# Sliding-window decode attention with a gated MLP: a quarter of the last Wo head group loaded in nine partial-row transfers, and the copy of x loaded on SyncE's queue

## The chip, the cores and the metric

The kernel runs on one core of one Trainium2 chip. The metric is device time in microseconds (us) of one launch. The kernel before was timed in three runs: 198.23, 198.25 and 198.52 us, median 198.25. The profile that is read below comes from one further execution, which took 198.21 us.

## The reference

One decode step for a batch of 8 rows of width 512. The input is normalised, goes through attention over the last 2048 positions of a key/value cache (32 query heads, 8 key/value heads of width 128) and, beside it, through a gated MLP of inner width 1792. The output is x + s * silu(b).

```python
xn = _layernorm(x, axis=-1)
# attention: W = min(4096, max(256, Sk // 4)) = 2048 of Sk = 8192
q = (xn @ wq).reshape(B, Sq, Hq, Dh)                 # 8 x 512 @ 512 x 4096
k, v = the last W positions of k_cache, v_cache, each head used by 4 query heads
p = softmax(q . k * Dh ** -0.5);  o = p . v
s = o.reshape(B, Sq, Hq * Dh) @ wo                   # 8 x 4096 @ 4096 x 512
# MLP
h = sigmoid(xn @ w_gate) * (xn @ w_up)
b = h @ w_down
out = x + s * silu(b)
```

Everything is bf16 in memory. Keys and values of the window are 32 MB each, the weights wq and wo 4 MB each, the MLP's three weights 1.75 MB each: about 81 MB are read for 8 KB of output.

## The kernel before, in words

**Loads.** All large loads go through `load` (line 88), which issues a DMA on SyncE's queue (`nc.sync`, SP in the profile). Keys and values come in tiles of 2 MB (`load_kv`, line 110), 16 of each; the query weights in two tiles; the MLP's in three. All of them live in a ring of nine buffers (`ring`, `RING = 9`). The list `loads` (lines 138 to 146) fixes their order: keys in the order of use, each value tile a lag behind its keys, the MLP's gate and up weights ahead of the last two tiles, and at the end the down weight and the two halves of Wo, `(2, 2), (3, 0), (3, 1)`. `issue_loads` (line 164) walks this list and stops where the buffer of nine places earlier is not in `released` yet. It is called after each step of the main loop, so a transfer is issued on the chip when the work on the buffer's former contents has ended.

**Marks of the transfers.** The framework gives each DMA that SyncE or ScalarE issues one of eight semaphores (marks) in turn: the first is `x_bf` on ScalarE's queue, then the loads on SyncE's, at the end the two stores of the output, one on each queue. A transfer that takes a mark waits, on the queue that issues it, until the transfer that had the mark before has landed. So each transfer waits for the one eight places earlier. DMAs of GpSimd's queue have marks of their own.

**Wo.** `wo_view` (line 149) has eight head groups (`hg`), 128 rows (`p`) and four quarters (`j`) of 512 columns: one row of one quarter is 1 KB, one quarter of a head group 128 KB. `load_wo` (line 152) loads the first half as two pieces of two head groups (1 MB each) and the second as head groups 4, 5 and 6 (512 KB each), quarters 0 and 1 of head group 7 (256 KB), quarter 2 (128 KB) and quarter 3 (128 KB), in this order.

**The copy of x.** `x2_sb` (line 181) is a 64 x 256 tile in the layout of the last sum: GpSimd clears it and then issues two DMAs of 8 rows by 512 B on its own queue (line 184), near the kernel's start.

**The end.** The main loop (line 610) interleaves the scores, softmax and value products of the 16 tiles. After it come the last sums of heads, `o_rows(1)`, the MLP's output product (`unit_out`, line 338) and the product with Wo (line 658 on): `order` runs through the head groups and their quarters, for each two matmuls (one for each half of the columns) accumulate into `a_ps`. VectorE then multiplies with the gate (`prod`, line 673) and adds `x2_sb` (`y_bf`, line 675), and two DMAs store the output (line 677). At the very end SyncE waits for all marks one after the other and a barrier follows (line 706 in the profile, the end of the context).

Of the kernel before, what the change touches and what calls it, by code (L numbers as in the profile page):

```python
# [10 lines left out]
def kernel(  # L11
# [13 lines left out]
    nc = tc.nc  # L25
    P = 128
    B, _, D = A_x.shape
# [9 lines left out]
    HG = Hq // 4  # L37
# [24 lines left out]
    NCOL = 2  # L62
    DC = D // NCOL

    bf16 = mybir.dt.bfloat16
# [8 lines left out]
    work = ctx.enter_context(tc.tile_pool(name="work", bufs=1))  # L74
# [13 lines left out]
    def load(dst, src, q=None):  # L88
        if q is None:
            q = nc.sync  # L90
        q.dma_start(out=dst, in_=src)

    def ring_tile(shape, name):
        return ring.tile(shape, bf16, name=name, tag="ring", align_bytes=ALIGN)

    x_bf = work.tile([B, D], bf16, name="x_bf")
    nc.scalar.dma_start(out=x_bf[:], in_=A_x.flatten_outer_dims())

# [3 lines left out]
    for kh in range(2):  # L102
        t = ring_tile([P, KH, Hq * Dh], f"wq_sb{kh}")
# [45 lines left out]
    wo_view = A_wo.rearrange("(hg p j) n -> p hg j n", p=P, j=4)  # L149
    wo_parts = {}  # L150

    def load_wo(half):
        t = ring_tile([P, HG // 2, 4, D], f"wo_sb{half}")
        for h0, h1, j0, j1 in (
            ((0, 2, 0, 4), (2, 4, 0, 4)),
            ((4, 5, 0, 4), (5, 6, 0, 4), (6, 7, 0, 4), (7, 8, 0, 2), (7, 8, 2, 3), (7, 8, 3, 4)),
        )[half]:
            o = half * (HG // 2)
            load(t[:, h0 - o : h1 - o, j0:j1, :], wo_view[:, h0:h1, j0:j1, :])
            for hg in range(h0, h1):  # L160
                for j in range(j0, j1):
                    wo_parts[hg, j] = t[:, hg - o, j, :]

    def issue_loads():
        while loads_done[0] < len(loads):
            n = loads_done[0]
            if n >= RING and loads[n - RING] not in released:
                break
            kind, i = loads[n]
            if kind == 0:  # L170
                k_tiles[i] = load_kv(A_k_cache, i, "k_sb")
            elif kind == 1:
                v_tiles[i] = load_kv(A_v_cache, i, "v_sb")
            elif kind == 2:
                load_mlp(i)
            else:
                load_wo(i)
            loads_done[0] += 1

    issue_loads()  # L180
    x2_sb = work.tile([NCOL * 32, DC], bf16, name="x2_sb")
    nc.gpsimd.memset(x2_sb[:], 0.0)
    for j in range(NCOL):
        nc.gpsimd.dma_start(
            out=x2_sb[32 * j : 32 * j + B, :],
            in_=A_x.flatten_outer_dims()[:, DC * j : DC * (j + 1)],
        )

    ident = consts.tile([P, P], bf16, name="ident")
    make_identity(nc, ident[:])  # L190
# [18 lines left out]
        out=rstd[:], in_=mv[:, 1:2], func=AF.Sqrt, bias=eps_t[:], scale=1.0  # L209
# [4 lines left out]
        out=xn_bf[:],  # L214
# [7 lines left out]
    for kt in range(KT):  # L222
        nc.tensor.transpose(
            out=xnT_ps[:, kt, :], in_=xn_bf[:B, kt::KT], identity=ident[:B, :B]
# [8 lines left out]
    for off in range(-rep * (NQ - 1), rep * NQ, rep):  # L233
        nc.gpsimd.affine_select(
            out=SumM[:],
            in_=SumM[:],
# [9 lines left out]
        out=SumM_blk,  # L246
        in_=SumM_blk,
# [7 lines left out]
        out=SumM_blk,  # L255
        in_=SumM_blk,
# [11 lines left out]
        out=Jneg[:],  # L268
        in_=ident[:].rearrange("p (a j r) -> p j a r", j=NQ, r=rep),
# [4 lines left out]
        out=Jneg[:], in0=Jneg[:], scalar1=-scale, scalar2=None, op0=ALU.mult  # L274
# [4 lines left out]
        out=Hm[:],  # L279
        in_=ident[:].rearrange("p (a gl) -> p gl a", gl=GL),  # L280
# [5 lines left out]
    for w in (32, 64):  # L286
        Sel[w] = consts.tile([P, w], f32, name=f"Sel{w}")
        nc.vector.tensor_reduce(
            out=Sel[w][:],
            in_=ident[:].rearrange("p (a m) -> p m a", m=w),  # L290
# [7 lines left out]
    for Q in range(NQ):  # L298
        nc.vector.tensor_copy(
            out=spread[:, :, Q, 32 * Q : 32 * (Q + 1)].rearrange(  # L300
                "m c (k g) -> m c g k", g=GL
            ),
            in_=ident[:].rearrange("m (g c k) -> m c g k", c=C4, k=KQ),
# [353 lines left out]

    a_ps = psum.tile([NCOL * 32, DC], f32, name="a_ps", tag="wide")
    order = [(hg, j) for hg in range(HG) for j in range(4)]
    for n, (hg, j) in enumerate(order):  # L660
        for c in range(NCOL):
            nc.tensor.matmul(  # L662
                a_ps[32 * c : 32 * (c + 1), :],
                lhsT=o2_sb[:, hg, j, :],
                rhs=wo_parts[hg, j][:, DC * c : DC * (c + 1)],
                start=(n == 0),
                stop=(n == len(order) - 1),
                tile_position=(0, 32 * c),
                skip_group_check=True,
            )  # L670
# [5 lines left out]
    for c in range(NCOL):  # L676
        queues[c].dma_start(
            out=out.flatten_outer_dims()[:, DC * c : DC * (c + 1)],
            in_=y_bf[32 * c : 32 * c + B, :],
# [31 lines left out]
```

## Time and profile before

| what | us |
|---|---|
| median of three runs | 198.25 |
| the profiled execution | 198.21 |
| its span, first to last instruction | 196.5 |
| the rest, outside the span | 1.7 |
| busy: TensorE matmuls | 138.2 |
| busy: VectorE | 117.0 |
| busy: ScalarE | 32.6 |
| busy: GpSimd | 9.3 |
| DMA from 13 to 155 us: share of the 16 engines, rate | 1.01, 430 GB/s |
| DMA from 183 to 193 us | 0.91, 363 GB/s |

A busy time is the sum over an engine's own work; the DMA share is the mean over the core's 16 DMA engines, and a share of 1 over a stretch says that none of them stood idle in it. The chain is the path of releases followed back from the last instruction. Issuing a DMA takes time on the queue of the engine that issues it (SPq for SyncE's), which is not counted as busy. Beside the views, the trace holds a record of each DMA packet (its start, duration and size) and the moment of each increment of a transfer's mark: a transfer over 128 rows increments its mark 16 times, once for each of the 16 engines, and has landed with the last.

### The profile page before, as it was taken

Reading aid. Unit: us, or ns where it says so; the run is one execution under the profiler, and the core shown is the slowest. Engines: PE = TensorE matmul, PEld = TensorE weight load, DVE = VectorE, ACT = ScalarE, POOL = GpSimd, SP = SyncE. Lnnn points to the kernel's source line nnn. Section 1 sums busy time; section 2 is a strip of 40 time slices with the busy share of each in tenths; the row PEclk is TensorE's granted clock in tenths of the full one; section 3 lists DMA queues with packets and bytes.
Section 4 is the critical chain, followed back from the end, with each engine's and each line's share of the span. In section 5 each row is a group of like instructions: output and inputs, shape, how many; then the busy total and the mean of one; then the engine's idle time right before and its main releaser. Section 6 shows DMA issues by size and latency. Waiting matters only on the chain.

```text
span 196.5 us, 2699 instructions
## 1 busy us (share of the span) xinstructions
PE 138.2 (70%) x1112; PEld 57.6 (29%) x1112; DVE 117.0 (60%) x200; ACT 32.6 (17%) x68; POOL 9.3 (5%) x21
## 2 busy tenths in 40 slices
PE   0340078669998987899789278946794779674783
PEld 0110011032324222423333044404240424443661
DVE  3818999746686828664777277837773750361101
ACT  3008540410121102101210021002100210340000
POOL 8820000000000000000000000000000000000000
PEclk9999999955999997879999957996888587996579
DMA  6999999999999999999999999999999999999991
GB/s 215 429 427 427 430 434 429 440 434 427 434 427 434 427 427 427 430 434 430 430 434 434 424 427 440 430 425 427 430 434 430 427 431 434 423 424 420 411 391 41
DMA packets 6860, 81.19 MB, mean 413 GB/s; under 512 B 792, under 2 KB 1088, under 8 KB 2112
## 3 DMA queue, kind: packets, MB, share of 16 engines
q1 hardware_dynamic: 6752, 81.01, 97.1%
q8 instruction: 8, 0.13, 0.2%
q10 hardware_dynamic: 32, 0.01, 0.1%
q14 instruction: 4, 0.03, 0.0%
q0 software_dynamic: 64, 0.01, 0.0%
HBM read 81.02 MB, written 0.01 MB: 412 GB/s over the span
## 4 chain that ended last, share of the span: by engine, by line
DMA 72%; DVE 17%; PE 8%; ACT 1%; issue 1%; SPq 0%; DVEq 0%; ACTq 0%
DMA k_sb<-in_A_k_cache_dram 47%; DMA wd_sb<-in_B_w_down_dram 14%; DVE k_sb L422 11%; DMA wq_sb<-in_A_wq_dram 6%; DMA wo_sb<-in_A_wo_dram 5%; PE pT_ps L486 3%; PE s_ps L435 3%; DVE qz_sb L395 2%; PE acc_ps L549 1%; DVE mx L447 1%; DVE qT_sb L386 1%; DVE pt_bf L475 1%; ACT L461 1%; PE q_ps L367 1%; PE mb_ps L456 0%
## 5 line engine op out<-in xcount | busy, mean ns | idle before, releaser
L422 DVE STREAM_TRANSPOSE k_sb<-k_sb 128x1024 f32<-128x1024 f32 x64 | 75.9, 1219 | 16.6 <-DMA k_sb<-in_A_k_cache_dram 16.5
L435 PE MATMUL s_ps<-k_sb,qz_sb 128*32 128x512 bf16 x256 | 68.7, 1065 | 16.4 <-DVE k_sb L422 11.6
L549 PE MATMUL acc_ps<-v_sb,pT_sb 128*32 128x256 bf16 (+1 forms) x416 | 35.3, 345 | 3.9 <-DMA v_sb<-in_A_v_cache_dram 2.6
L549 PEld LDWEIGHTS <-pT_sb 128*32 128x32 bf16 (+1 forms) x416 | 12.5, 109 | 33.2 <-issue 27.0
L506 DVE TENSOR_SCALAR pT_sb<-pc_bf,Hm 128x512 bf16<-128x512 bf16 x32 | 9.1, 349 | 18.3 <-ACT pc_bf L495 18.3
L435 PEld LDWEIGHTS <-qz_sb 128*32 128x32 bf16 x256 | 8.3, 100 | 34.0 <-issue 26.1
L560 ACT COPY acc_sb<-acc_ps 128x256 f32<-128x256 f32 (+1 forms) x16 | 7.2, 453 | 63.2 <-PE acc_ps L549 63.2
L486 PE MATMUL pT_ps<-pt_bf,spread 128*128 128x128 bf16 x128 | 12.5, 272 | 6.3 <-DVE pt_bf L475 6.3
L570 PEld LDWEIGHTS oT_ps<-Sel,acc_sb 128*128 128x128 f32 x88 | 11.8, 202 | 14.3 <-ACT acc_sb L560 8.5
L570 PE MATMUL oT_ps<-Sel,acc_sb 128*128 128x16 f32 x88 | 13.4, 276 | 1.1 <-ACT acc_sb L560 1.1
L486 PEld LDWEIGHTS <-spread 128*128 128x128 bf16 x128 | 10.8, 123 | 10.8 <-DVE pt_bf L475 10.8
L456 PE MATMUL mb_ps<-mj,SumM 128*128 128x4 f32 x16 | 3.5, 286 | 14.3 <-DVE mj L449 14.3
L461 ACT ACTIVATE p_bf<-s_ps,nm 128x512 bf16<-128x512 f32 x8 | 5.5, 687 | 46.5 <-DVE nm L458 46.5
L577 DVE TENSOR_TENSOR oT_sb<-oT_ps,rden 128x16 bf16<-128x16 f32 x16 | 2.6, 160 | 11.7 <-PE oT_ps L570 11.7
L456 PEld LDWEIGHTS mb_ps<-mj,SumM 128*128 128x128 f32 x16 | 2.8, 218 | 22.5 <-DVE mj L449 20.6
L397 ACT COPY qz_sb<-qT_sb 32x128 bf16<-32x128 bf16 x20 | 8.3, 413 | 3.0 <-DVE qT_sb L386 2.7
L530 DVE RECIPROCAL rden<-den_ps 128x32 f32<-128x32 f32 x8 | 2.8, 351 | 7.3 <-PE den_ps L528 7.3
L495 ACT CAST pc_bf<-pT_ps 128x512 bf16<-128x512 f32 x8 | 4.7, 587 | 13.1 <-PE pT_ps L486 13.1
L367 PE MATMUL q_ps<-wq_sb,xnT_sb 128*32 128x512 bf16 x32 | 3.8, 625 | 4.0 <-DMA wq_sb<-in_A_wq_dram 4.0
L475 DVE STREAM_TRANSPOSE pt_bf<-p_bf 128x512 bf16<-128x512 bf16 x8 | 5.4, 679 | 1.9 <-ACT p_bf L461 1.9
L662 PE MATMUL a_ps<-wo_sb,o_sb 128*32 128x256 bf16 x64 | 5.5, 315 | 1.0 <-DMA wo_sb<-in_A_wo_dram 0.9
L447 DVE TENSOR_REDUCE mx<-s_ps 128x1 f32<-128x512 f32 x8 | 5.3, 657 | 0.0
(61 smaller groups left out, 61.9 us busy)
## 6 DMA issues: line engine op xcount, KB each, us to landing
k_sb<-in_A_k_cache_dram SPq DMA_DIRECT2D x16, 2048.0 KB, 31.8
v_sb<-in_A_v_cache_dram SPq DMA_DIRECT2D x16, 2048.0 KB, 29.5
wq_sb<-in_A_wq_dram SPq DMA_DIRECT2D x2, 2048.0 KB, 9.7
wo_sb<-in_A_wo_dram SPq DMA_DIRECT2D x2, 1024.0 KB
wg_sb<-in_B_w_gate_dram SPq DMA_DIRECT2D x1, 1792.0 KB, 29.3
wu_sb<-in_B_w_up_dram SPq DMA_DIRECT2D x1, 1792.0 KB, 30.1
wd_sb<-in_B_w_down_dram SPq DMA_DIRECT2D x1, 1792.0 KB, 27.6
wo_sb<-in_A_wo_dram SPq DMA_DIRECT2D x3, 512.0 KB, 23.5
```

The costliest lines, as they stand in the source:

```text
L397: nc.scalar.copy(out=out, in_=in_)
L422: nc.vector.transpose(out=kw, in_=kw)
L435: nc.tensor.matmul(s_tiles[b][32 * gl : 32 * (gl + 1), :], lhsT=qz_sb[:, b, GL * gg + gl, j, :], rhs=kT[:, :, a, :, gl, e], start=(gg == 0 ...
L447: nc.vector.reduce_max(out=mx[:], in_=s_tiles[b][:], axis=AX.X)
L456: nc.tensor.matmul(mb_ps[:], lhsT=SumM[:], rhs=mj[:], start=True, stop=True)
L461: nc.scalar.activation(out=p_bf[:], in_=s_tiles.pop(b)[:], func=AF.Exp, bias=nm[:], scale=scale, accum_out=den128[:],)
L475: nc.vector.transpose(out=pt_bf[:].rearrange("p c g q r -> p (c g q r)"), in_=p_bf[:])
L486: nc.tensor.matmul(pT_ps[:, :, c4, :], lhsT=spread[:, c4, Q, :], rhs=pt[:, :, Q, :], start=(Q == 0), stop=(Q == NQ - 1), skip_group_check= ...
L506: nc.vector.tensor_scalar(out=pT_tiles[b][:, :, gl, :], in0=pc, scalar1=Hm[:, gl : gl + 1], scalar2=None, op0=ALU.mult,)
L549: nc.tensor.matmul(acc_tiles[i][w * c : w * (c + 1), :], lhsT=pT[:, 32 * y : 32 * y + w], rhs=v_tiles[i][:, ch : ch + n_ch, :].rearrange(" ...
L560: nc.scalar.copy(out=acc_sb[:], in_=acc_tiles.pop(i)[:])
L570: nc.tensor.matmul(oT_ps[:], lhsT=acc_sb[:, Dh * c : Dh * (c + 1)], rhs=sel[:, c // 2, c % 2], start=(c == 0), stop=(c == n_ch - 1),)
```

## The change

Quarter 2 of head group 7 (128 rows of 1 KB) is no longer one transfer after head group 7's first half. It is cut into nine transfers of 64, 14, 12, 10, 8, 8, 6, 4 and 2 rows. Three of them follow head group 4, three head group 5 and three head group 6. Quarters 0 and 1 and then quarter 3 of head group 7 are the last two pieces. The product with Wo takes head group 7's quarters in the order 2, 0, 1, 3. The two DMAs of `x2_sb` move from GpSimd's queue at the start to SyncE's queue, between the two pieces of Wo's first half; GpSimd still clears the tile, now as its first work.

```diff
+    x2_sb = work.tile([NCOL * 32, DC], bf16, name="x2_sb")
+    nc.gpsimd.memset(x2_sb[:], 0.0)
     x_bf = work.tile([B, D], bf16, name="x_bf")
...
+    def load_x2():
+        for j in range(NCOL):
+            load(
+                x2_sb[32 * j : 32 * j + B, :],
+                A_x.flatten_outer_dims()[:, DC * j : DC * (j + 1)],
+            )
+
+    PARTS = (64, 14, 12, 10, 8, 8, 6, 4, 2)
+
     def load_wo(half):
         t = ring_tile([P, HG // 2, 4, D], f"wo_sb{half}")
-        for h0, h1, j0, j1 in (
-            ((0, 2, 0, 4), (2, 4, 0, 4)),
-            ((4, 5, 0, 4), (5, 6, 0, 4), (6, 7, 0, 4), (7, 8, 0, 2), (7, 8, 2, 3), (7, 8, 3, 4)),
-        )[half]:
-            o = half * (HG // 2)
-            load(t[:, h0 - o : h1 - o, j0:j1, :], wo_view[:, h0:h1, j0:j1, :])
-            for hg in range(h0, h1):
-                for j in range(j0, j1):
-                    wo_parts[hg, j] = t[:, hg - o, j, :]
+        h_lo = half * (HG // 2)
+
+        def piece(h0, h1, j0, j1, r0=0, r1=P):
+            load(
+                t[r0:r1, h0 - h_lo : h1 - h_lo, j0:j1, :],
+                wo_view[r0:r1, h0:h1, j0:j1, :],
+            )
+
+        if half == 0:
+            piece(0, 2, 0, 4)
+            load_x2()
+            piece(2, 4, 0, 4)
+        else:
+            r0 = 0
+            for n, rows in enumerate(PARTS):
+                if n % 3 == 0:
+                    h = h_lo + n // 3
+                    piece(h, h + 1, 0, 4)
+                piece(HG - 1, HG, 2, 3, r0, r0 + rows)
+                r0 += rows
+            assert r0 == P
+            piece(HG - 1, HG, 0, 2)
+            piece(HG - 1, HG, 3, 4)
+        for h in range(h_lo, h_lo + HG // 2):
+            for j in range(4):
+                wo_parts[h, j] = t[:, h - h_lo, j, :]
...
-    x2_sb = work.tile([NCOL * 32, DC], bf16, name="x2_sb")
-    nc.gpsimd.memset(x2_sb[:], 0.0)
-    for j in range(NCOL):
-        nc.gpsimd.dma_start(
-            out=x2_sb[32 * j : 32 * j + B, :],
-            in_=A_x.flatten_outer_dims()[:, DC * j : DC * (j + 1)],
-        )
...
     order = [(hg, j) for hg in range(HG) for j in range(4)]
+    order[-4:] = [(HG - 1, j) for j in (2, 0, 1, 3)]
```

## The prediction

> **What bounds the kernel now.** I read the page's rows of slices first, then the chain, then the stretches and waits of its end.
>
> The slices show DMA full from the second to the last but one:
>
> ```profile
> DMA  6999999999999999999999999999999999999991
> GB/s 215 429 427 427 430 434 429 440 434 427 434 427 434 427 427 427 430 434 430 430 434 434 424 427 440 430 425 427 430 434 430 427 431 434 423 424 420 411 391 41
> ```
>
> So the time is 81 MB at about 430 GB/s, plus what follows the last byte. The chain, from 155 us on, says which bytes count:
>
> ```profile
> 155.44 27.61 DMA wd_sb<-in_B_w_down_dram
> 183.06 9.89 DMA wo_sb<-in_A_wo_dram
> 192.95 0.04 issue
> 192.99 0.30 PE a_ps L662 x2
> 193.29 0.02 issue
> 193.32 0.42 DVE prod L673
> 193.74 0.02 issue
> 193.76 0.28 DVE y_bf L675
> ```
>
> The down weight lands at 183.05, the last quarter of Wo at 192.95; two matmuls and two VectorE operations follow, the stores are issued at 194.07, and the span ends at 196.5. Only three things can change the time: when the last piece of Wo lands, what TensorE has left then, and what follows the stores.
>
> Issues on SyncE's queue, taken from its timeline in narrow windows, show how the tail is fed:
>
> ```profile
> 165.58 0.82 SPq L91 DMA_DIRECT2D wo_sb<-in_A_wo_dram  x2
> 169.08 4.22 SPq L91 DMA_DIRECT2D wo_sb<-in_A_wo_dram  x1
> 173.93 3.39 SPq L91 DMA_DIRECT2D wo_sb<-in_A_wo_dram  x1
> 178.77 1.52 SPq L91 DMA_DIRECT2D wo_sb<-in_A_wo_dram  x1
> 183.06 0.33 SPq L91 DMA_DIRECT2D wo_sb<-in_A_wo_dram  x1
> ```
>
> The last four issues begin when the up weight, the last two value tiles and the down weight have landed (169.06, 173.92, 178.76, 183.05 by the records): each waits for the mark of the transfer eight places earlier. Here that costs nothing, since 9.9 us of data still lie ahead.
>
> Last, the 16 increments of each mark. The last quarter's come in two groups: seven engines at 191.18 to 191.64, nine at 192.54 to 192.95. The queues' rows show what makes engines late:
>
> ```profile
> q1 hardware_dynamic: 6752, 81.01, 97.1%
> q8 instruction: 8, 0.13, 0.2%
> ```
>
> Eight instruction loads of 16 KB (44, 67, 94, 111, 131, 151, 172 and 182 us) each hold one engine for 0.88 to 0.97 us and lengthen its next packet by about half a microsecond. After each, one more increment of every transfer comes about 1.4 us late. The end is set by the nine late engines.
>
> **The change part by part.** The sum starts from the profiled execution: 198.21 us, of which 196.50 span and 1.71 outside, 0.04 below the median of 198.25.
>
> *x2 off GpSimd's queue.* GpSimd loses two issues (0.65 and 0.52, 1.17 us from 1.41 us on); its setup moves up by as much. It is idle after 13 us, and the first product waits for the query weights at 13.1, so this gains nothing, and costs nothing. ScalarE's queue is not touched. The 16 packets of 512 B (27 ns each, 9 ns a completion) leave the stream at 6 us and return at 185 us: at most two rows and two completions on one engine, 0.07, out and in: 0.
>
> *x2 on SyncE's queue.* Two issues between Wo's first pieces. What waits behind them is the second piece, issued at 159.26 now. It, and the two issues, move three marks along: the second piece now waits for the gate weights (landed 164.67), head group 4 for the up weight (169.06), the next three transfers for 173.92, 178.76 and 183.05. Data issued before 155.5 lasts to 183.05, so all of this is covered. If that cover were gone, each issue would cost about 0.45.
>
> *Rows of the nine transfers.* By the packet records a 1 KB packet takes 46 ns and a completion 9. `x_bf`, 8 rows, left eight 1 KB packets and eight completions, so I take it that a transfer of fewer than 16 rows gives an engine at most one. The 64 rows give each engine four, the other eight transfers between zero and eight more, against eight now. On the engine that ends last that is -4 to +4 rows, -0.18 to +0.18, and up to eight more completions, +0.07. Nine engines of 16 are late, so a well-served one is probably among them: near the upper end, I take +0.20 between -0.18 and +0.26.
>
> The Trainium skill, page "DMA: Bandwidth & Descriptors", section on why a DMA increments its semaphore by 16, says more: from SyncE's queue a copy uses the largest number of engines up to 16 that divides its rows, always the lowest-numbered ones. By that, engines 0 and 1 get 12 rows and 14 and 15 get 4, and the sum would have +0.26 if engine 0 or 1 is late, and about -0.1 if only upper ones are. No view shows which engines are late.
>
> *Feeding the tail.* This is the part that could cost most. In places of eight, head group 5 now waits for Wo's first piece (185.44), head group 6 for head group 4, head group 7's first half for head group 5, its last quarter for the ten-row transfer. On the late engines head group 4 lands at 189.2 (189.14 now, plus x2's 0.07). SyncE then issues six in a row: head group 6, the 6, 4 and 2 rows, the first half, the last quarter. An issue of such shapes takes 0.33 to 0.43, and 0.05 lie between two, so the first half is issued four steps of 0.38 to 0.48 later, at 190.8 to 191.2. From issue to first packet an idle path took 0.79 (store, 194.07 to 194.86) to 1.04 (first weights, 0.81 to 1.85), so its data can start at 191.6 to 192.2. The late engines are free for it at about 192.0 (191.65 now is when head group 6 lands, 0.3 after its last packet; plus x2, plus up to 12 rows and nine completions less the last). Head group 6 itself, issued at 189.25, is ready at 190.3 and needed at 190.6. So the stall is 0 to 0.2; with the 0.69 of the first key issues as a step it would be 1.0. I take 0.1, near the rows of like shapes, and keep 0 to 1.0. The early engines will stand idle, which costs nothing, since they have 1.4 us to give.
>
> The same page's rules for authors say that transfers under 64 KB are mostly overhead and that two halves of the partitions should go as one transfer; its fit of 2.0 us a transfer would make nine of them about 18 us by themselves. The records here charge 9 ns a completion on an engine that has a queue, so I keep the sum above.
>
> *TensorE.* Head group 7's quarter 2 has nine transfers on six marks, so more waits stand ahead of its two matmuls: a wait instruction of TensorE took 0.05, three to five of them 0.15 to 0.25. Eight matmuls took 0.61 (at 190.45) and a pair follows a pair by 0.11. From head group 6's landing to the last one there are 1.0 to 1.3 us; 0.61, 0.25 and three pairs (0.33) make 1.2. I take +0.05, between 0 and 0.3. VectorE's wait for x2 just moves to two other marks that landed by 186.
>
> *After the stores.* The records have SyncE's seven wait instructions at the end at 194.90, 194.98, 195.05, 195.12, 195.19, 195.37 and 195.54, in the order of the marks from the second to the eighth, 0.07 apart unless one waits. The stores are the 47th and 48th transfers with such marks, so they have the seventh and eighth, landed at 195.35 and 195.53, and nothing follows but the barrier. The change adds eight pieces and two x2 transfers: the stores become 57th and 58th, with the first and second marks. If the order of waits stays, the wait of 195.53 comes first, and five more steps of 0.07 stand behind it: +0.35. If the order goes by age, 0, or -0.07 as GpSimd's two marks are gone. The order is by number as much as by age in this trace; I take +0.35 and keep -0.07.
>
> Sum: 198.21 + 0.20 + 0.10 + 0.05 + 0.35 = 198.9 us.
>
> **The rivals.**
> *Waits at the end keep the stores last* (order by age). For it: in this trace both orders agree. The sum is then 198.21 + 0.35 = 198.56, inside what a measurement can tell (0.2%, 0.4 us).
> *SyncE starves the tail.* For it: six issues in a row hang on one landing, and the first issues of this kernel took 0.63 to 0.69. Against it: rows of the same shapes took 0.33 to 0.43. Steps of 0.6 or a first packet after 1.3 us put the first half 0.4 to 1.0 late: 199.2 to 199.9.
> *The nine transfers relieve the late engines* (the other side). One mechanism: rows move from engines that an instruction load held to engines that none held. It decides if all nine late engines get at most seven rows, which spares 46 ns a row, -0.05 to -0.18, with the waits at the end unmoved and the tail fed: 198.0 to 198.2, not slower. Against it: nine late engines cannot all have fewer than eight rows unless seven take the rest, and the unevenness to be gained from is only the 0.41 within the late group. A fall of over 0.4 needs more than four rows can give.
>
> **How the numbers follow.** The forecast 0.45 (198.6 to 199.1), the tail starved 0.20 (199.2 to 199.9), the stores' waits unmoved 0.23 (198.3 to 198.6), relief 0.12 (197.8 to 198.2). Slower by over 0.2% (above 198.65) takes nearly all of the first and the second: 0.65. Within 0.2%: 0.29. Faster: half of relief's doubtful part, 0.06. The range runs from 198.1, where relief ends, to 199.7; cut off are about one in ten at each end.
>
> **What would show it.** If the steps are right, the last 16 increments of Wo come in a closer group, at 193.2 to 193.4; SyncE's issues of head group 6 and five more stand in a row from about 189.3, 0.4 to 0.5 apart; the two matmuls of the last quarter follow its landing within 0.1; and five wait instructions stand between the stores' landing and the barrier. Wrong it is if DMA's last landing is at 192.9 or earlier (relief), if DMA has a gap near 192 (starving), or if the barrier follows the stores' landing as closely as now.

## The result and the profile after

The changed kernel takes 199.95 us (median of five runs, 199.54 to 200.08) against 198.41 before (five runs, 198.23 to 198.64). The ratio is 1.0075 with a 95% interval of 1.0057 to 1.0092: about 1.5 us slower, outside the predicted range. The direction was right; the size was 2.2 times what the sum gave (1.54 against 0.70). The ratios here and below leave out executions in a slower state, of which the series had one (207.87 us, with the even parts early).

The profiled execution's span is 197.9 us, 1.4 longer than before. The last two slices of the page's DMA rows have changed:

```profile
DMA  6999999999999999999999999999999999999971
GB/s 217 427 437 434 444 427 422 424 431 431 434 440 427 424 427 431 427 437 437 424 431 431 427 427 437 437 419 431 434 427 424 432 431 433 424 431 408 413 259 54
```

The last slice but one fell from 391 to 259 GB/s. The DMA view from 184 to 196 us, 0.3 us a slice, shows where. First before, then after:

```profile
DMA  9999999999999999999999976565100000001010
GB/s 396 423 437 423 396 423 423 437 396 423 423 423 423 423 410 437 423 396 396 430 410 372 406 283 236 212 212 201 51 0 0 0 0 0 0 0 28 0 27 0
```

```profile
DMA  9999899999999998865416579996798840000000
GB/s 382 410 417 413 369 410 437 437 423 396 396 427 406 410 410 314 304 249 232 171 48 116 109 300 410 355 423 110 191 300 331 311 150 0 0 0 0 0 0 0
```

Before, the stream is full to about 191 us and then falls to about half, because seven engines are done early. After, it thins from 188.5, is nearly dry from 190.0 (48 GB/s, then 116 and 109 until 190.9), full again from about 191.1, and has a second hole at 192.1 (110 GB/s). By the packet records the engines' idle time between 183 us and Wo's last packet grew from 8.1 to 21.4 engine-us, 0.83 us for each of the 16. Some packets also took longer: over the usual 159 ns for 4 KB and 84 ns for 2 KB, Wo's packets from 183 us on took 0.50 us more on each engine, against 0.03 before. All but 0.05 of this lies between 190 and 193 us, in the holes and right behind them. The two together (0.83 + 0.47) are about what the last landing is late.

The chain now runs through SyncE's issues:

```profile
169.02 20.44 DMA wo_sb<-in_A_wo_dram
189.46 0.02 issue
189.48 0.35 SPq L91
189.83 0.04 issue
189.88 0.32 SPq L91
190.20 0.05 issue
190.25 0.29 SPq L91
190.53 0.04 issue
190.58 0.25 SPq L91
190.83 0.04 issue
190.88 3.02 DMA wo_sb<-in_A_wo_dram
193.89 0.04 issue
193.94 0.63 PE a_ps L684 x6
```

Head group 4 is issued at 169.02 and lands at 189.46. Only then is head group 6 issued (189.48), as its mark is head group 4's; the 6, 4 and 2 rows and the first half of head group 7 (190.88) follow one by one. The landings on the last engine, from the increments of the marks:

| piece of Wo | before, us | after, us | later by |
|---|---|---|---|
| first piece (1 MB) | 185.44 | 185.33 | -0.11 |
| head group 4 | 189.14 | 189.46 | 0.32 |
| head group 5 | 190.41 | 190.65 | 0.24 |
| head group 6 | 191.65 | 192.87 | 1.22 |
| head group 7, first half | 192.28 | 193.89 | 1.61 |
| the last quarter | 192.95 | 194.22 | 1.27 |

The first hole is the step of 0.98 between head groups 5 and 6, the second the 0.39 after it; the last quarter gains 0.34 back, since no other quarter stands before it. From the last landing to the stores' issue it took 1.12 before and 1.13 after. The later store landed 1.46 and 1.47 after its issue. From there to the span's end it is 0.97 before and 1.06 after. Together: 1.27 + 0.01 + 0.01 + 0.09 = 1.38, the growth of the span (196.50 to 197.88).

### The profile page after: what moved, and what is told of

It is laid out like the page before. It is cut to its first block, busy times and chain, and to the rows that moved or that the text cites. A ratio compares the mean times of both kernels' runs of the same rounds, so it can differ in the third digit from the quotient of the medians.

```text
span 197.9 us, 2709 instructions
## 1 busy us (share of the span) xinstructions
PE 142.6 (72%) x1112; PEld 59.3 (30%) x1112; DVE 117.1 (59%) x200; ACT 32.5 (16%) x68; POOL 7.7 (4%) x19
## 4 chain that ended last, share of the span: by engine, by line
DMA 64%; DVE 17%; PE 14%; ACT 2%; SPq 1%; issue 1%; DVEq 0%; ACTq 0%
DMA k_sb<-in_A_k_cache_dram 31%; DMA wu_sb<-in_B_w_up_dram 15%; DMA wo_sb<-in_A_wo_dram 12%; DVE k_sb L443 11%; DMA wq_sb<-in_A_wq_dram 6%; PE s_ps L456 6%; PE pT_ps L507 3%; PE acc_ps L570 3%; DVE qz_sb L416 2%; DVE mx L468 1%; SPq L91 1%; DVE qT_sb L407 1%; DVE pt_bf L496 1%; ACT L482 1%; DVE pT_sb L527 1%
## 5 line engine op out<-in xcount | busy, mean ns | idle before, releaser
L570 PE MATMUL acc_ps<-v_sb,pT_sb 128*32 128x256 bf16 (+1 forms) x416 | 36.5, 365 | 1.3 <-DVE pT_sb L527 1.3
L507 PE MATMUL pT_ps<-pt_bf,spread 128*128 128x128 bf16 x128 | 13.2, 281 | 6.5 <-DVE pt_bf L496 6.5
L591 PEld LDWEIGHTS oT_ps<-Sel,acc_sb 128*128 128x128 f32 x88 | 12.9, 219 | 15.0 <-ACT acc_sb L581 9.1
L591 PE MATMUL oT_ps<-Sel,acc_sb 128*128 128x16 f32 x88 | 14.5, 290 | 1.1 <-ACT acc_sb L581 1.1
L507 PEld LDWEIGHTS <-spread 128*128 128x128 bf16 x128 | 11.3, 128 | 10.8 <-DVE pt_bf L496 10.8
L684 PE MATMUL a_ps<-wo_sb,o_sb 128*32 128x256 bf16 x64 | 4.9, 307 | 1.8 <-DMA wo_sb<-in_A_wo_dram 1.8
```

The costliest lines, as they stand in the source:

```text
L507: nc.tensor.matmul(pT_ps[:, :, c4, :], lhsT=spread[:, c4, Q, :], rhs=pt[:, :, Q, :], start=(Q == 0), stop=(Q == NQ - 1), skip_group_check= ...
L570: nc.tensor.matmul(acc_tiles[i][w * c : w * (c + 1), :], lhsT=pT[:, 32 * y : 32 * y + w], rhs=v_tiles[i][:, ch : ch + n_ch, :].rearrange(" ...
L591: nc.tensor.matmul(oT_ps[:], lhsT=acc_sb[:, Dh * c : Dh * (c + 1)], rhs=sel[:, c // 2, c % 2], start=(c == 0), stop=(c == n_ch - 1),)
L684: nc.tensor.matmul(a_ps[32 * c : 32 * (c + 1), :], lhsT=o2_sb[:, hg, j, :], rhs=wo_parts[hg, j][:, DC * c : DC * (c + 1)], start=(n == 0), ...
```

## The experiments

The theory after seeing this: the change's ten further transfers use up the eight marks, so that the tail's pieces are issued after the landing of a piece only one or two places ahead in the stream, and the DMA engines run dry (theory of the marks). Rivals: the two transfers of x on SyncE's queue, the uneven rows on engines that are late already, and a price of each small transfer wherever it stands. Each run is compared with the kernel before on the same chip.

**The parts alone.** The copy of x back on GpSimd's queue:

```diff
                 A_x.flatten_outer_dims()[:, DC * j : DC * (j + 1)],
+                q=nc.gpsimd,
...
             piece(0, 2, 0, 4)
-            load_x2()
             piece(2, 4, 0, 4)
...
     issue_loads()
+    load_x2()
```

> The copy of x goes back to GpSimd's queue at the start; the nine transfers stay where the change put them. Marks (the tail is starved because each transfer waits for the one eight places earlier): head group 6 still waits for head group 4 to land, with the same six issues behind it, so the hole in the DMA stream near 190 us stays; only the stores get the seventh and eighth marks again, worth about 0.2. Expected 199.6 to 199.9 us against 198.4 before. Rival (the two x transfers on SyncE's queue are what costs): back to 198.4 to 198.7.

Measured: 199.8 us, ratio 1.0054 (1.0033 to 1.0076). Head group 6 was issued at 189.43, when head group 4 landed, the hole is there and Wo landed at 194.53, 1.58 later than before. The nine transfers make the loss.

**x alone.** Wo's second half in the old six pieces:

```diff
...
+            for h in (4, 5, 6):
+                piece(h, h + 1, 0, 4)
             piece(HG - 1, HG, 0, 2)
+            piece(HG - 1, HG, 2, 3)
             piece(HG - 1, HG, 3, 4)
...
-    order[-4:] = [(HG - 1, j) for j in (2, 0, 1, 3)]
```

> Only the copy of x moves to SyncE's queue; Wo's second half is loaded in the six pieces of before, in their order. Marks: head group 6 waits for the last value tile, head group 7's pieces for the down weight (183.1), Wo's first piece and the first x transfer (185.5), all more than 5 us ahead of their need, so Wo lands at 192.9 to 193.1 as before. The stores become the 49th and 50th transfers with the first and second marks, which puts five more wait steps behind them: +0.2 to +0.35. Expected 198.5 to 198.8. Rival (x on SyncE's queue costs): 199.5 or more.

Measured: 198.36 us, ratio 0.9994 (0.9979 to 1.0009): no difference. Wo landed at 193.00. The waits did move as expected: the stores got the first two marks, and four wait steps, 0.06 apart, stood between their landing (195.59) and the barrier. But the expected 0.2 to 0.35 is a miss: the whole way from the stores' landing to the span's end is only 0.10 longer than before (1.07 and 0.97), because there are four steps of 0.06, not five of 0.07, and the barrier behind the last of them was over after 0.76 (195.84 to 196.60) in place of 0.90 (195.54 to 196.44).

**Even parts.** The same count at the same places, with even rows:

```diff
-    PARTS = (64, 14, 12, 10, 8, 8, 6, 4, 2)
+    PARTS = (16, 16, 16, 16, 16, 16, 16, 8, 8)
```

> The change with the nine transfers cut to 16, 16, 16, 16, 16, 16, 16, 8 and 8 rows at the same places, so that every engine gets seven to nine of the 128 rows. Marks: the number and the places of the transfers are the same, so the hole stays: 199.6 to 200.1. Rival (the uneven rows load the late engines): at least the quarter of a microsecond that up to four more rows and the completions cost comes back, and if rows were the whole cause, 198.4 to 198.7.

Measured: 200.41 us, ratio 1.0094 (1.0067 to 1.012). Not faster than the uneven parts, so the unevenness is not what costs. Head group 6 was issued at 189.51 and the hole is the same.

**The parts on GpSimd's queue**, which has marks of its own:

```diff
...
-                piece(HG - 1, HG, 2, 3, r0, r0 + rows)
+                piece(HG - 1, HG, 2, 3, r0, r0 + rows, nc.gpsimd)
```

> The change with the nine transfers issued on GpSimd's queue, which has marks of its own; the copy of x stays on SyncE's queue. Marks: on SyncE's queue the last quarter waits for Wo's first piece (185.4), nothing in the tail waits for less than 5 us ahead, so Wo lands at 192.9 to 193.3: 198.3 to 198.8. Rival (nine small transfers are dear by themselves, or their rows are badly spread): 199.4 or more, as after the change.

Measured: 199.94 us, ratio 1.0072 (1.0044 to 1.01): the time of the change, against the expectation. But it is lost elsewhere. The tail has no hole: from the landing of Wo's first piece (187.41) to the last quarter's (194.57) it takes 7.16 us, where before it took 7.51 with the quarter's 0.33 in it. The profiled execution, the longest of the six (200.7 us), loses its time earlier: that first landing is 1.97 us later than before, of which 0.3 is the quarter's own data, now ahead of it. About 0.9 of the rest goes between 165 and 182 us, while GpSimd's small transfers run between the large ones; where the other 0.8 goes isn't worked out. The stretches of this run, then of the kernel before:

```profile
165.00:182.00 17.00, 11.24 (x176) 7.10 (x176) 5.99 (x16) 3.98 (x8) 4.65 (x9) 0.85 1.02 403
```

```profile
165.00:182.00 17.00, 11.54 (x195) 7.39 (x188) 6.11 (x16) 4.57 (x9) 0.00 (x0) 0.90 1.00 426
```

The last two columns are the DMA share and GB/s: as busy as before, but slower. From 13 to 190 us 155 packets of 16 KB took over 640 ns, where 611 is usual; before there were 9. So this run took the hole away and brought in a cost of its own; it doesn't separate the theories by its time.

**The parts early.** A tile of their own, one part behind each of nine key and value loads:

```diff
...
+    wq2_sb = work.tile([P, D], bf16, name="wq2_sb")
...
             loads_done[0] += 1
+            if 12 <= n < 12 + len(PARTS):
+                load_part(n - 12)
```

> The same nine transfers, in a tile of their own, one behind each of nine key and value loads in the first half of the kernel; Wo's tail then is head groups 4, 5, 6, the first half of head group 7 and its last quarter. Marks: the tail's issues wait for landings more than 5 us ahead of the need, so no hole near 190 us: 198.2 to 198.6. Rival (nine small transfers cost by their number, wherever they stand): 199.2 or more. Relief of the late engines by the uneven rows, if it exists, shows here undisturbed: at most 0.2 below before.

Measured: 200.17 us, ratio 1.009 (1.0063 to 1.0116). A miss, and for the rival at first sight. There is no hole in the tail here either: head group 6 was issued at 180.88, and its data landed 12.96 us later behind the pieces ahead of it. The loss lies where the small transfers are. The stretches of this run, then of the kernel before:

```profile
20.00:62.00 42.00, 31.77 (x170) 9.42 (x170) 33.03 (x48) 10.17 (x21) 0.00 (x0) 0.92 1.01 430
62.00:112.00 50.00, 44.49 (x274) 15.68 (x273) 30.78 (x48) 5.45 (x11) 0.00 (x0) 0.83 1.01 416
112.00:155.00 43.00, 30.01 (x254) 13.45 (x258) 27.51 (x44) 4.22 (x10) 0.00 (x0) 0.76 1.01 431
```

```profile
62.00:112.00 50.00, 42.25 (x276) 14.70 (x274) 31.20 (x49) 5.46 (x11) 0.00 (x0) 0.93 1.01 430
```

From 62 to 112 us the engines are fully busy but move 416 in place of 430 GB/s, which is 1.6 us in 50. By the packet records 328 packets of 16 KB took over 640 ns (9 before), mostly around and after a small transfer. The excess over 611 ns, from 13 to 190 us, is 1.82 us for each engine, against 0.27 before. So this is a third price, which the theory of the marks doesn't have. The change can't have paid it in this form: in the changed kernel 9 packets of 16 KB are long, as before, for its small transfers move when no such packets are left. What they do to the smaller packets of the tail is told with the three and six parts.

**Even parts early:**

> As the run with the nine transfers early, but with 16, 16, 16, 16, 16, 16, 16, 8 and 8 rows. If uneven rows relieve the late engines, this one is 0.05 to 0.2 slower than the uneven one; if they load them, as much faster; if rows don't matter, the two agree within 0.1. Expected 198.2 to 198.6.

Measured: 200.09 us (199.97 without the one of 207.87), ratio 1.0083 (1.0062 to 1.0104), with 391 long packets; some stretches between two small transfers ran at a nearly constant 720 ns (68 to 70 us) or 682 ns (74 to 77 us) a packet. Even and uneven rows don't differ.

**The whole quarter early**, one transfer of 128 rows in that tile:

```diff
+    PARTS = (128,)
```

> The quarter as one transfer of 128 rows in a tile of its own, behind one key tile in the first half of the kernel. In the runs with nine transfers there the 16 KB packets around and between them took 640 to 720 ns in place of 611, and the stream lost 1.8 us. If that comes with each small transfer, one of them costs a ninth: 198.3 to 198.5. If it comes with any interruption of the row of large tiles and stays: 199 or more.

Measured: 198.9 us, ratio 1.0023 (1.0005 to 1.0042), with 29 long packets; the 20 more than before lie between 60 and 80 us. It is above the expected 198.3 to 198.5 and below the 199 of a price that stays: after 80 us the packets are as before. Wo landed at 193.44, 0.49 later; why one transfer costs that much isn't shown.

**Three parts** in the tail, and **six**, which tell the marks from the number:

```diff
-    PARTS = (64, 14, 12, 10, 8, 8, 6, 4, 2)
+    PARTS = (64, 32, 32)
...
-    PARTS = (64, 14, 12, 10, 8, 8, 6, 4, 2)
+    PARTS = (64, 16, 16, 16, 8, 8)
...
```

One part stands behind each of head groups 4, 5 and 6 in the first run, two in the second.

> The change with the quarter in three transfers (64, 32 and 32 rows), one behind each of head groups 4, 5 and 6. Marks: head group 6 now waits for Wo's first piece (185.4) and the last quarter for Wo's second piece (188.0), both over 2 us ahead of the need, so there is no hole: 198.3 to 198.7. Rival (cutting the quarter into row parts among the large pieces is dear in itself): a third of the loss or more, 198.9 to 199.2.

> The quarter in six transfers (64, 16, 16, 16, 8 and 8 rows), two behind each of head groups 4, 5 and 6. Marks: head group 6 waits for the second x transfer (185.5) and head group 7's first half for the 64 rows (189.4, issued near 189.7, needed at 192.0), so there is no hole: 198.4 to 198.9. Rival (each cut costs the same): from 198.6 with three to 199.95 with nine transfers, half way, 199.2 to 199.4.

Measured: three parts 198.64 us, ratio 1.0019 (1.0003 to 1.0035); six parts 198.47 us, ratio 1.0016 (0.9993 to 1.0039). Six cost no more than three, and nine cost 1.0075: not a price for each, but a threshold. With six, head group 6 was issued at 186.59, behind the second transfer of x and not behind head group 4:

```profile
186.21 0.33 SPq L91
186.53 0.06 issue
186.59 5.59 DMA wo_sb<-in_A_wo_dram
192.18 0.04 issue
```

The DMA view from 184 to 196 us is full to 190.0. Then the early engines alone wait for head group 7's first half (issued at 189.89), until 190.9, while the late ones are at work:

```profile
DMA  9999999999999999999967699985400000000100
GB/s 410 437 415 401 437 437 437 423 396 386 413 399 410 423 434 396 376 362 396 372 260 284 259 375 341 321 314 215 140 7 0 0 0 0 0 0 5 22 0 0
```

In both runs Wo landed at 193.19, 0.24 later than before; with x alone it was 193.00. Wo's packets are a little long here too: the excess over 159 and 84 ns is 0.18 us on each engine with three parts and 0.22 with six. So perhaps 0.2 of the change's 1.27 comes with the cutting itself, and about 1.0 with the holes.

**The parts together**, all nine behind head group 4:

> The change with all nine transfers directly behind head group 4, so that 5, 6 and the rest of 7 come after them. Marks: the eighth and ninth of them wait for head group 4 and for the first of the nine to land (189.3 to 189.6), and everything behind stands in SyncE's queue until then; the stream is dry from about 189.7, head group 5 starts at about 191.2 and Wo lands at 194.9 to 195.4: 200.2 to 201.0, slower than the change. Rival (only the number of transfers counts): 199.9, as the change.

Measured: 201.55 us, ratio 1.0169 (1.0148 to 1.0189): more than expected. Head group 5 was issued at 189.96, when everything ahead of it had nearly landed, and the stream stood nearly still for six slices, 1.8 us:

```profile
DMA  9999999999976553100000089999989999996200
GB/s 396 398 418 423 423 437 437 410 423 403 393 304 253 218 205 120 51 0 0 0 3 17 0 164 341 341 396 369 369 341 423 423 382 266 331 379 212 68 0 0
```

The same nine transfers, moved so that the waits fall worse, cost 2.2 times as much.

**The marks alone.** Eight dummy transfers of one row (512 B, into a tile that nothing reads) at the places of the first eight, and the quarter whole at the ninth:

```diff
+    dummy = work.tile([8, DC], bf16, name="dummy")
...
+            for n in range(9):
+                if n % 3 == 0:
+                    h = h_lo + n // 3
+                    piece(h, h + 1, 0, 4)
+                if n < 8:
+                    load(dummy[n : n + 1, :], A_x.flatten_outer_dims()[n : n + 1, :DC])
+                else:
+                    piece(HG - 1, HG, 2, 3)
```

> The change's places without its cutting: eight dummy transfers of one row of 512 B (into a tile that nothing reads) stand where the first eight of the nine stood, and the quarter goes as one transfer of 128 rows at the ninth place. Marks: head group 6 still waits for head group 4 with six issues in a row from 189.4, so the stream runs dry near 190 us and again near 192 just the same: 199.4 to 200.0. Rival (small pieces of rows cost by the way they disturb the stream): most of the loss goes, 198.4 to 198.9.

Measured: 199.86 us, ratio 1.0076 (1.0051 to 1.0102), the ratio of the change. The chain is that of the change as well:

```profile
168.92 20.18 DMA wo_sb<-in_A_wo_dram
189.10 0.02 issue
189.11 0.35 SPq L91
189.47 0.04 issue
189.51 0.28 SPq L91
189.79 0.05 issue
189.84 0.25 SPq L91
190.08 0.04 issue
190.13 0.35 SPq L91
190.48 0.04 issue
190.52 3.70 DMA wo_sb<-in_A_wo_dram
```

4 KB of dummies in the right places are enough (the quarter as a whole at the ninth place leaves some 0.3 us more of data behind the wait than the change does, so that the two ratios agree this closely is partly chance). With the six parts this settles the main cause: the loss is in how many transfers stand between a piece and the one whose mark it takes over.

No version beat the kernel before; the nearest are x alone (0.9994) and six parts (1.0016).

## Why the prediction was wrong

*What bounds the kernel* was right: only the last landing of Wo, TensorE's rest and the way after the stores count, and the 1.38 splits into these three, with 1.27 on the first.

*x2 on SyncE's queue*, costed at nothing: right, 0.9994 alone. Each mark moved as listed; the cover of data held.

*Rows*, costed at +0.20 within -0.18 to +0.26: the unevenness doesn't show. Even rows were not faster, in the tail or early. The 0.19 between x alone and the three or six parts, whose rows are even or nearly so, is of the size forecast, but goes with longer packets and not with uneven rows. What the rows were said to be is right: the 14-row transfer added 14 increments to its mark beside one update 0.5 us after its issue, the 12-row one 12. The Trainium skill says this in "DMA: Bandwidth & Descriptors", section on why a DMA increments its semaphore by 16: a copy whose rows admit only k engines gets k increments from them, and the issuing sequencer writes the other 16 - k at once. The trace agrees with k; of the update at issue it shows the moment and not the size. It also speaks against relief: of the 16 increments of the 64 rows seven are early and nine late, of the 14-row transfer's six and eight, of the 12-row one's six and six. So three of the four engines with the fewest rows were late. But of the eight increments of the first x transfer three are late as well (185.16 to 185.51), and by the rule in that section of the Trainium skill that the lowest-numbered engines are taken, the engines of an eight-row transfer get nine rows or more of the quarter. That rival's condition did not hold.

*Feeding the tail*, +0.10 within 0 to 1.0, is the step that failed. It reckoned one stall of 0 to 0.2 at head group 7's first half, found head group 6 in time, and put the idle time of the early engines at nothing; there were two holes, of 0.98 at head group 6 and 0.39 at the first half. The mechanism was named, with the right pieces (head group 6 behind head group 4, six issues in a row) and nearly the right steps: the issues began 0.30 to 0.40 apart (0.38 to 0.48 expected), the first half at 190.88 where 190.8 to 191.2 was expected. Three terms inside it were off. First, the landing of head group 4 was taken as 189.2 and was 189.46; why is open. Second, the need was reckoned for the engine with the most rows (free at 190.6); the engines that get nothing of the small transfers have only head group 5 and were free from 190.0, and the early ones from 188.6. All sixteen were busy again at 191.1 only, so the early engines' 1.4 us were lost too and head group 6 came in on all of them at once (192.45 to 192.87). Third, the time from issue to first packet was read from the first packet of any engine (and its 0.79 joins SyncE's issue to a packet of ScalarE's store; SyncE's own first packet came 0.84 after). For head group 6 that was right (189.48 to 190.46, 0.98), but the 16 engines' first packets are spread: full activity came 1.6 us after the issue. For the first half of head group 7, issued fifth in the row, the first packet came 1.33 us after its issue (190.88 to 192.21) and most engines had data again only at 192.6, which made the second hole; some of its 2 KB packets took up to 442 ns in place of 84. The sum had no term for such packets.

The last increments of Wo came as one close group, as forecast, but at 193.77 to 194.22 in place of 193.2 to 193.4.

The same page of the Trainium skill also says, in its section on the anatomy of one DMA, that "DMA engines do not wait on semaphores": a wait happens on the issuing sequencer before dispatch. That fits the holes: nothing is prepared while SyncE waits, and the whole way from issue to the last engine's first packet is paid after each landing.

*TensorE*, +0.05: 0.01. The extra waits stayed covered.

*After the stores*, +0.35: the waits went in the order of their numbers, as taken, but the way from the last landing to the end grew by 0.09, and in the run of x alone by 0.10: four waits stood there, not five, and a shorter barrier gave back most of their time. So it is partly luck that the direction was right: 0.55 of the 0.70 forecast stood on the uneven rows and on these waits.

*The rivals.* "SyncE starves the tail" is what happened, at 0.20 chance and 199.2 to 199.9, just under the measured 199.95; of its two conditions the first packet after 1.3 us came true, at the first half, and the steps of 0.6 did not. The other two did not come about. The 2.0 us a transfer that the prediction took from the Trainium skill and set aside is given there ("DMA: Bandwidth & Descriptors", the anatomy of one DMA) for GpSimd's queue; nine transfers on SyncE's cost 1.5 us in all, and six 0.3. The larger chance was put on "slower", which came true; the price of the rival that hung on one landing should have been worked out for every engine, not for the busiest.

## What to carry to other kernels

Count transfers, not bytes, when the queue of outstanding DMAs is limited: with eight marks in turn a transfer of one row holds back the piece eight places later as much as a megabyte does, so small transfers in a tail must leave at least the issue-to-data time (here 1.6 us until the last engine was busy) of streaming between a piece and the landing it waits for. Check that for the engine with the least work, as it runs dry first. A cut that stays under that threshold is nearly free in this tail (three and six parts), one over it is paid at once.

## What the runs showed of the hardware

Small transfers among a saturated row of 2 MB loads slow the large packets beside them: nine of them took the rate from 430 to 416 GB/s over 50 us at an unchanged DMA share of 1.01, with 328 packets of 16 KB mostly at 650 to 700 ns in place of 611 and, with even rows, steady stretches at 682 and 720 ns. One whole 128-row transfer left 29 such packets. On GpSimd's queue, from 165 to 182 us, nine took the rate from 426 to 403 GB/s. In the tail, where the packets are of 4 and 2 KB, the eight dummies with the whole quarter and the six parts left some long ones too, on each engine 0.39 and 0.22 us over the usual times of 4 and 2 KB packets, against 0.03 before. What makes the packets longer, and why the length stays constant between two disturbances, is open; nothing here tells a changed phase between the engines from another cause.
